# Running two gate/up blocks ahead of the first down phase, putting a state phase on 64-column halves of the array, and cutting the last tile pair in three

## Chip, cores, metric

One core of one Trainium2 chip. The metric is the device time of one execution in microseconds, median over executions; "span" is the time from the first to the last instruction in a profile, about 1.3 to 1.6 us less.

## The reference

`x` is 2048 x 640 in bfloat16; 32 heads of 20.

```python
q, k, v = split_heads(x @ wqkv)                       # 32 heads of 20
phi_q = concat(softmax(q @ w_phi), softmax(-(q @ w_phi)))
phi_k = concat(softmax(k @ w_phi), softmax(-(k @ w_phi)))
kv  = einsum("hsf,hsd->hfd", phi_k, v)                # "gram": summed over all 2048 tokens
z   = phi_k.sum(tokens)
a   = ((phi_q @ kv) / (phi_q @ z + 1e-6)) @ wo        # numerator over denominator
b   = (gelu(x @ w_gate) * (x @ w_up)) @ w_down        # 640 -> 1728 -> 640
g   = sigmoid(x . gate_w)
out = g * a + (1 - g) * b
```

## The kernel before

Tokens go in 16 tiles of 128, or 4 blocks of 512. There are three kinds of work on TensorE:

1. The state phase: for each tile t, project v and k (`vk`), exponentiate k on ScalarE, normalise it on VectorE (`k_norm`), and add the tile's outer product to the state (`gram`); between these, project q (`pq`).
2. Gate/up, 14 chunks per block: two chains of five 512-column matmuls into a pair of PSUM banks; gelu on ScalarE, product `hT` on VectorE.
3. Down, two tiles at a time, on the two 64-row halves of the array, with the attention numerators (`num(t)`, also on 64-row halves) in between. Each `num` takes 0.39 us of TensorE and then a chain of ten VectorE operations, which must end before the next `num` may write the same four banks.

The gram multiplies `vaug` (v with a column of ones, 21 columns per head) by both exponentials. Only the blocks on the diagonal (a head with itself) are wanted:

```python
def gram_groups(self):              # six groups of six heads, 126 of 128 columns used
    fe = 6 * self.DH
    for g in range(6):
        lo = min(6 * g * self.DA, self.H * self.DA - P)
        yield g, 3 + g % 2 if g < 4 else 5, 2 * fe * (g // 2 if g < 4 else g - 4), lo, fe * g, min(fe, self.D - fe * g)

def gram(self, t):
    ...
    for g, b, c, lo, f0, nf in self.gram_groups():
        sc.op("pe", lambda e: e.matmul(
            self.bank(b)[:, c:c + 2 * nf], va[:, lo:lo + P], self.Ek[:, se, :, f0:f0 + nf], ...))
```

The order of the second half (cut):

```python
early = {8: 0, 10: 1, 12: 2}                       # numerators inside gate/up of block 0
side = [{20: 3, 72: 4, 98: 5, 124: 6, 148: 7}, {40: 8, ...}, ...]   # inside the down phases
for b in range(self.NB):
    for idx, c in enumerate(order):
        self.gateup(b, c, ...)
        if b == 0:
            if idx == 0: self.gram(14)
            if idx == 3: self.gram(15); self.kv_evac(); self.gates()
            if idx == 6: self.kv_mask()
            if idx in early: self.num(early[idx])
    for t in (4 * b, 4 * b + 2):
        for step in self.down_pair(t, p, b == 0):
            if n in side[b]: self.num(side[b][n])
            step()
            n += 1
```

The state is copied out of PSUM (`kv_evac`), transposed by DMA, and spread into block-diagonal form by 4 copies and 15 multiplications on VectorE (`kv_mask`) before `num(0)`.

The softmax here doesn't subtract the row's maximum and nothing guards it: scores larger than these inputs give would overflow.

## Time and profile before

| | |
|---|---|
| time, median of 3 fast runs (of 4) | 296.9 us |
| span of the profiled run | 294.6 us |
| TensorE busy | 98% |
| VectorE / ScalarE busy | 56% / 36% |
| granted TensorE clock | 1.00 |

The head of the profile page: span, then busy time, share and instructions of each engine ("PEld" is weight loading, which overlaps "PE").

```profile
span 294.6 us, 6191 instructions
...
PE 288.2 (98%) x2608; PEld 165.5 (56%) x2608; DVE 165.6 (56%) x331; ACT 105.8 (36%) x197; POOL 27.7 (9%) x52
```

The groups of instructions with shapes kept apart, gram alone. Columns: line, engine, operation, operands, rows*columns of the array, shape, count | busy us, mean ns of one | idle before.

```profile
L441 PE MATMUL ps<-Ek,vaug 128*128 128x240 bf16 x80 | 10.7, 266 | 0.0
L441 PEld LDWEIGHTS ps<-Ek,vaug 128*128 128x128 bf16 x96 | 9.3, 98 | 2.1
L441 PE MATMUL ps<-Ek,vaug 128*128 128x80 bf16 x16 | 3.2, 199 | 0.0
```

A matmul's recorded length overlaps its neighbours, so cost is read from the distance of starts. This is the TensorE timeline before (start us, length us, engine, line, operation, count).

```profile
50.01 1.26 PE L441 MATMUL ps<-Ek,vaug 128*128 128x240 bf16 x12
...
59.23 0.71 PE L441 MATMUL ps<-Ek,vaug 128*128 128x240 bf16 x6
59.78 1.24 PE L505 MATMUL ps<-xT,wq 128*128 128x512 bf16 x5
60.86 2.87 PE L348 MATMUL ps<-w,xT 128*128 128x512 bf16 x15
63.57 0.71 PE L441 MATMUL ps<-Ek,vaug 128*128 128x240 bf16 x6
```

One gram costs 59.78 - 59.23 = 0.55 us, five 512-column matmuls 60.86 - 59.78 = 1.08 us (216 ns each), a whole tile 63.57 - 59.23 = 4.34 us. The x12 at 50.01 is grams 5 and 6 in a row, so gram 6 starts near 50.55. The VectorE timeline at the same time:

```profile
46.77 1.48 DVE L418 TENSOR_REDUCE Dk<-Ek 128x64 f32<-128x1280 bf16 x1
48.28 0.55 DVE L422 RECIPROCAL Dk<-Dk 128x64 f32<-128x64 f32 x1
48.87 1.56 DVE L427 TENSOR_TENSOR Ek<-Ek,Dk 128x640 bf16<-128x640 bf16 x2
50.35 1.48 DVE L418 TENSOR_REDUCE Dk<-Ek 128x64 f32<-128x1280 bf16 x1
```

Normalisation 6 ends near 50.4 us (48.87 + 1.56), less than 0.2 us before gram 6 begins, and the next one starts at once: VectorE is back to back here, 3.58 us per tile. The waits of TensorE (waiter <- awaited: us in total, times, longest):

```profile
PE ps L533 <- DVE zero L529: 1.3, 1, 1.3
PE ps L646 <- DVE O L673: 1.1, 3, 0.6
PE ps L700 <- DVE hT L618: 0.4, 1, 0.4
PE ps L505 <- ACT Eq L511: 0.3, 1, 0.3
PE ps L646 <- DVE KV L496: 0.3, 1, 0.3
```

The first is the start-up; the others are in block 0 (L646 is `num`, L700 is down), but for one in the state phase. By windows, the stretch from the first gram (29.40 us) to the end splits so. Columns: window, its length, busy us and instructions of PE, PEld, DVE, ACT and POOL, then the granted clock, the busy share of the DMA engines and the GB/s that they moved:

```profile
29.40:82.54 53.14, 53.14 (x331) 31.12 (x330) 49.06 (x56) 39.13 (x78) 0.00 (x0) 1.00 0.34 110
82.54:140.26 57.72, 55.68 (x604) 31.50 (x602) 42.07 (x115) 14.93 (x27) 8.79 (x7) 1.00 0.17 36
140.26:191.28 51.02, 51.02 (x515) 29.15 (x511) 23.25 (x55) 11.51 (x22) 6.56 (x5) 1.00 0.12 27
...
291.82:294.60 2.78, 0.01 (x2) 0.00 (x0) 0.55 (x1) 0.53 (x1) 0.00 (x0) 1.00 0.22 59
```

They are the state phase, block 0, block 1 and the tail after the last matmul. Block 0 takes 6.7 us more than block 1, which has neither its extra numerators, its two grams nor its waits.

### The profile page before, as it was taken

The page shows a single profiled execution, that of the slowest core. Times are in us where ns is not written, and L with a number is a line of the kernel's source. Part 1 is how long each engine was busy: PE and PEld are TensorE (multiplying, and loading weights), DVE is VectorE, ACT ScalarE, POOL GpSimd, SP SyncE. Part 2 cuts the span into 40 slices and gives each one's busy share as a digit, 9 for nine tenths or more (in the row PEclk, how much of TensorE's full clock was granted, in tenths as well). Part 3 has the DMA queues.
Part 4 walks back from the last instruction along what each step waited for, and adds up shares of the span by engine and source line. Part 5 has one row for each costly group of instructions (what it writes and reads, how often), then busy time and mean ns, then how long its engine had stood idle before and what let it go on. Part 6 is the DMA issues. An engine that isn't in the chain of part 4 may idle for free.

```text
span 294.6 us, 6191 instructions
## 1 busy us (share of the span) xinstructions
PE 288.2 (98%) x2608; PEld 165.5 (56%) x2608; DVE 165.6 (56%) x331; ACT 105.8 (36%) x197; POOL 27.7 (9%) x52
## 2 busy tenths in 40 slices
PE   8999999999999999998999999999999999999996
PEld 4675656555554444765444477744447764444774
DVE  3258999998875799458733227473237743323000
ACT  3368787586664221021322302132320223232012
POOL 7000000000000012312300001310001230000000
PEclk9999999999999999999999999999999999999999
DMA  8999992000002102113210001230000132000011
GB/s 226 213 185 313 359 346 84 0 0 2 0 2 55 34 2 46 24 24 91 78 15 0 0 2 24 70 89 2 0 0 20 29 70 67 2 0 0 2 47 45
DMA packets 38373, 18.93 MB, mean 64 GB/s; under 512 B 30154, under 2 KB 38090, under 8 KB 38346
## 3 DMA queue, kind: packets, MB, share of 16 engines
q1 hardware_dynamic: 37392, 18.11, 24.5%
q10 hardware_dynamic: 954, 0.44, 0.6%
q8 instruction: 20, 0.33, 0.5%
q14 instruction: 7, 0.06, 0.1%
HBM read 9.04 MB, written 2.62 MB: 40 GB/s over the span
## 4 chain that ended last, share of the span: by engine, by line
PE 55%; DVE 7%; issue 2%; ACT 0%; DVEq 0%
PE ps L613 29%; PE ps L700 23%; DVE O L673 2%; PE ps L646 2%; PE ps L623 1%; DVE hT L618 1%; DVE RH L667 1%; DVE RH L662 1%; DVE RH L668 1%; DVE RH L665 0%; DVE RH L663 0%; DVE RH L664 0%; DVE RH L666 0%; DVE RH L669 0%; ACT outsb L726 0%
## 5 line engine op out<-in xcount | busy, mean ns | idle before, releaser
L618 DVE TENSOR_TENSOR hT<-ps,gl 128x512 bf16<-128x512 f32 x52 | 35.6, 690 | 55.8 <-PE ps L613 55.6
L613 PE MATMUL ps<-xT,wg_sb 128*128 128x512 bf16 x260 | 64.7, 379 | 0.0
L613 PE MATMUL ps<-xT,wu_sb 128*128 128x512 bf16 x260 | 64.6, 379 | 0.0
L700 PE MATMUL ps<-wd_sb,hT 64*128 64x320 bf16 x864 | 64.0, 296 | 0.4 <-DVE hT L618 0.4
L616 ACT ACTIVATE gl<-ps 128x512 bf16<-128x512 f32 x52 | 31.1, 597 | 73.8 <-PE ps L613 67.7
L700 PEld LDWEIGHTS ps<-wd_sb,hT 64*128 64x128 bf16 x864 | 41.5, 94 | 18.1 <-ACT gl L616 0.8
L613 PEld LDWEIGHTS ps<-xT,wu_sb 128*128 128x128 bf16 x260 | 25.5, 98 | 30.6
L726 ACT ACTIVATE outsb<-ps,Gm 128x320 bf16<-128x320 f32 x31 | 14.6, 525 | 77.7 <-PE ps L700 77.6
L675 POOL TENSOR_TENSOR Og<-O,O 128x640 bf16<-128x640 bf16 x16 | 22.3, 1395 | 212.8 <-DVE O L673 212.8
L613 PEld LDWEIGHTS ps<-xT,wg_sb 128*128 128x128 bf16 x260 | 24.9, 98 | 29.4 <-issue 0.3
L348 PE MATMUL ps<-w,xT 128*128 128x512 bf16 (+3 forms) x240 | 40.9, 321 | 0.0
L348 PEld LDWEIGHTS ps<-w,xT 128*128 128x128 bf16 x240 | 22.4, 97 | 18.2
L700 PE MATMUL ps<-wo_sb,goT 64*128 64x320 bf16 x320 | 27.0, 296 | 0.0
L418 DVE TENSOR_REDUCE Dk<-Ek 128x64 f32<-128x1280 bf16 x16 | 23.7, 1481 | 3.2 <-ACT gcol L410 3.2
L427 DVE TENSOR_TENSOR Ek<-Ek,Dk 128x640 bf16<-128x640 bf16 x32 | 25.0, 821 | 0.6
L505 PE MATMUL ps<-xT,wq 128*128 128x512 bf16 x100 | 24.7, 379 | 0.3 <-ACT Eq L511 0.3
L673 DVE TENSOR_TENSOR O<-ps,RH 128x640 bf16<-128x640 f32 x32 | 24.8, 816 | 0.0
L511 ACT ACTIVATE Eq<-ps 128x512 bf16<-128x512 f32 x40 | 21.7, 604 | 4.0 <-PE ps L505 4.0
L407 ACT ACTIVATE Ek<-ps 128x640 bf16<-128x640 f32 x32 | 20.7, 702 | 3.5 <-PE ps L348 3.5
L662 DVE RECIPROCAL RH<-ps 128x32 f32<-128x32 f32 x16 | 5.7, 356 | 23.5 <-PE ps L646 23.5
L700 PEld LDWEIGHTS ps<-wo_sb,goT 64*128 64x128 bf16 x320 | 15.2, 94 | 5.7
L505 PEld LDWEIGHTS ps<-xT,wq 128*128 128x128 bf16 x100 | 8.8, 98 | 8.4 <-ACT Eq L511 0.8
(65 smaller groups left out, 150.2 us busy)
## 6 DMA issues: line engine op xcount, KB each, us to landing
out_dram<-outsb SPq DMA_DIRECT2D x14, 160.0 KB, 2.1
wd_sb<-in_B_w_down_dram SPq DMA_DIRECT2D x1, 2080.0 KB, 12.6
wg_sb<-in_B_w_gate_dram SPq DMA_DIRECT2D x1, 1120.0 KB, 6.1
wu_sb<-in_B_w_up_dram SPq DMA_DIRECT2D x1, 1120.0 KB, 9.5
wg_sb<-in_B_w_gate_dram SPq DMA_DIRECT2D x1, 960.0 KB, 9.6
wu_sb<-in_B_w_up_dram SPq DMA_DIRECT2D x1, 960.0 KB, 10.2
w<-in_A_wqkv_dram SPq DMA_DIRECT2D x5, 160.0 KB, 4.3
wo_sb<-in_A_wo_dram SPq DMA_DIRECT2D x1, 800.0 KB, 9.3
```

The costliest lines, as they stand in the source:

```text
L348: sc.op("pe", lambda e, kt=kt: e.matmul(self.bank(bank)[:, bcol:bcol + n], self.xT[:, kt, t * P:(t + 1) * P], self.w3[:, kt, c0:c0 + n], s ...
L407: self.sc.op("act", lambda e, s=s, scale=scale: e.activation(self.Ek[:, se, s, :], self.ps[:, o:o + self.D], AF.Exp, scale=scale), reads=[ ...
L418: sc.op("dve", lambda e: e.tensor_reduce(self.Dk[:, se, 0, :].rearrange("p (s h) -> p s h", h=H), self.Ek[:, se, :, :].rearrange("p s (h d ...
L427: sc.op("dve", lambda e, v=v, r=r: e.tensor_tensor(v, v, r, ALU.mult), reads=[("Rk", se)], writes=[("Ek", se, s)])
L505: sc.op("pe", lambda e, kt=kt: e.matmul(self.bank(bank), self.wq2[:, kt, i * P:(i + 1) * P], self.xT[:, kt, b * self.BT:(b + 1) * self.BT] ...
L511: sc.op("act", lambda e, s=s, scale=scale: e.activation(self.Eq[:, s, i, b * self.BT:(b + 1) * self.BT], self.bank(bank), AF.Exp, scale=sc ...
L613: sc.op("pe", lambda e, kt=kt, w=w, bk=bk: e.matmul(self.bank(bk), w[:, kt, c * P:(c + 1) * P], xs(kt), start=(kt == 0), stop=(kt == self. ...
L616: sc.op("act", lambda e: e.activation(self.gl[:, slot, :], self.bank(banks[0]), AF.Gelu_apprx_tanh), reads=[("ps", banks[0])], writes=[("g ...
L618: sc.op("dve", lambda e: e.tensor_tensor(self.hT[:, c, :], self.bank(banks[1]), self.gl[:, slot, :], ALU.mult), reads=[("ps", banks[1]), ( ...
L673: dve(lambda e, o=o, f=f, s=s: e.tensor_tensor(o, V[s][:, :, :, 0:DH], f, ALU.mult), rb + [key(6 + s)], [("O", s, sl)], guard=old)
L675: sc.op("pool", lambda e: e.tensor_tensor(self.Og[:, sl, :], self.O1[:, sl, :], self.O2[:, sl, :], ALU.add), reads=[("O", 0, sl), ("O", 1, ...
L700: sc.op("pe", lambda e: e.matmul(self.bank(bk, 320), lhs, rhs, start=first, stop=fin, skip_group_check=True), reads=rd, writes=[("ps", bk) ...
```

## The change

The intent: (a) a gram of narrower groups (three heads, 63 of 64 columns) does half the multiplications for blocks that nobody wants, if two such matmuls run at once on the two column halves of the array; (b) so that TensorE does not change its array mode between grams and projections, all projections of that stretch are cut into two 64-column halves too; (c) gate/up of blocks 0 and 1 both run before the first down phase (a second `hT`, laid over buffers of the state phase), so numerators need not be squeezed into down 0; (d) the last pair of tiles is finished in column parts of 256, 256 and 128 instead of 320 and 320, so that less is left to evict and store at the end.

```diff
+    def mm(self, bank, c0, n, lhs, rhs, first, fin, reads):
+        for a, z in ((0, 64), (64, P)) if self.columns else ((0, P),):
+            self.sc.op("pe", lambda e: e.matmul(
+                self.ps[a:z, bank * 512 + c0:bank * 512 + c0 + n], lhs[:, a:z], rhs, start=first, stop=fin),
+                reads=reads, writes=[("ps", bank)], signal=fin and z == P)
     def gram_groups(self):
-        fe = 6 * self.DH
-        for g in range(6): ...
+        fe = 3 * self.DH
+        for g in range(11):
+            u = g // 2
+            yield (g, 64 * (g % 2), 3 + u // 4, 2 * fe * (u % 4), min(3 * g * self.DA, self.H * self.DA - 64), fe * g,
+                   min(fe, self.D - fe * g))
     def gram(self, t):
-                self.bank(b)[:, c:c + 2 * nf], va[:, lo:lo + P], self.Ek[:, se, :, f0:f0 + nf],
+                self.ps[a:a + 64, b * 512 + c:b * 512 + c + 2 * nf], va[:, lo:lo + 64], self.Ek[:, se, :, f0:f0 + nf],
 ... kv_evac: one transpose instead of two; kv_mask: 20 multiplications instead of 15; proj and pq call mm ...
+        self.columns = True          # from the first gram to the end of the state phase
         self.gram(0)
 ... ffn ...
+        def state(idx):
+            if idx == 2: self.gram(14); self.gram(15); self.kv_evac(); self.gates()
+            if idx == 6: self.kv_mask()
+        def first_nums(idx):
+            if idx in (3, 6, 9, 12): self.num(idx // 3 - 1)
+        at = (8, 44, 80, 116)
+        gateups(0, state)
+        gateups(1, first_nums)
+        for b in range(self.NB):
+            downs(b, {at[k]: 4 * b + 4 + k for k in range(4)} if b < 3 else {})
+            if b < 2:
+                gateups(b + 2, none)
 ... downs, for the pair that is final ...
+                for _ in self.down_pair(t, p + [(2, 3)] if final else p, (256, 256, 128) if final else (320, 320)):
```

(The inner `if` lines are joined here. Outputs of two tiles now also leave in one DMA, and the special order of the first down phase, output projections last, is gone.)

More of the change, by code (lines that the diff above doesn't have):

```diff
@@ L134, in run @@
         self.alloc()
+        self.columns = False
         self.sc = _Sched(nc, {"sp": (nc.sync, 16), "act": (nc.scalar, 4), "pool": (nc.gpsimd, 2)})
@@ L151, in alloc @@
         self.Eq = T("Eq", [P, 2, KD, S], BF16)
-        self.Ek = T("Ek", [P, self.NSE, 2, D], BF16)
-        self.vaug = T("vaug", [P, self.NSV, self.H, self.DA], BF16)
-        self.Dk = T("Dk", [P, self.NSE, 2, 2 * self.H], F32)
         self.KV = T("KV", [P, KD, 2, self.HB * self.DB], BF16)
@@ L188, in alloc @@
             [("w3", [P, KD, 2 * D + 2], BF16), ("wq2", [P, KD, D], BF16)],
-            [("hT", [P, NFC, BT], BF16), ("gl", [P, 3, BT], BF16)],
+            [("hT0", [P, NFC, BT], BF16), ("gl", [P, 3, BT], BF16)],
+        ])
+        place([
+            [("Ek", [P, self.NSE, 2, D], BF16), ("vaug", [P, self.NSV, self.H, self.DA], BF16),
+             ("Dk", [P, self.NSE, 2, 2 * self.H], F32)],
+            [("hT1", [P, NFC, BT], BF16)],
         ])
@@ L343, in fold @@
             self.sc.op("act", lambda e: e.activation(dst, src, AF.Copy), reads=rd, writes=wr)
+    def mm(self, bank, c0, n, lhs, rhs, first, fin, reads):
[3 more added lines that the diff above has]
+                reads=reads, writes=[("ps", bank)], signal=fin and z == P)
     def proj(self, t, c0, n, bank, bcol, keys):
-        sc = self.sc
         for kt in range(self.KD):
-            sc.op("pe", lambda e, kt=kt: e.matmul(
-                self.bank(bank)[:, bcol:bcol + n], self.xT[:, kt, t * P:(t + 1) * P], self.w3[:, kt, c0:c0 + n],
-                start=(kt == 0), stop=(kt == self.KD - 1)),
-                reads=[("xT", t)] + [(k, kt) if k != "wgate" else k for k in keys],
-                writes=[("ps", bank)], signal=(kt == self.KD - 1))
+            self.mm(bank, bcol, n, self.xT[:, kt, t * P:(t + 1) * P], self.w3[:, kt, c0:c0 + n], kt == 0,
+                    kt == self.KD - 1, [("xT", t)] + [(k, kt) if k != "wgate" else k for k in keys])
     def v_step(self, t, kt):
@@ L430, in gram_groups @@
     def gram_groups(self):
-        fe = 6 * self.DH
-        for g in range(6):
-            lo = min(6 * g * self.DA, self.H * self.DA - P)
-            yield g, 3 + g % 2 if g < 4 else 5, 2 * fe * (g // 2 if g < 4 else g - 4), lo, fe * g, min(fe, self.D - fe * g)
+        fe = 3 * self.DH
[3 more added lines that the diff above has]
+                   min(fe, self.D - fe * g))
     def gram(self, t):
@@ L439, in gram, with copy @@
         va = self.vaug[:, sv, :, :].rearrange("p h c -> p (h c)")
-        for g, b, c, lo, f0, nf in self.gram_groups():
+        for g, a, b, c, lo, f0, nf in self.gram_groups():
             sc.op("pe", lambda e: e.matmul(
-                self.bank(b)[:, c:c + 2 * nf], va[:, lo:lo + P], self.Ek[:, se, :, f0:f0 + nf],
-                start=(t == 0 and g in (0, 1, 4)), stop=(t == self.NT - 1 and g in (2, 3, 5)), skip_group_check=True),
+                self.ps[a:a + 64, b * 512 + c:b * 512 + c + 2 * nf], va[:, lo:lo + 64], self.Ek[:, se, :, f0:f0 + nf],
+                start=(t == 0 and g in (0, 1, 8, 9)), stop=(t == self.NT - 1 and g in (6, 7, 9, 10)),
+                skip_group_check=True),
                 reads=[("Ek", se, 0), ("Ek", se, 1), ("vaug", sv), ("vmain", sv), ("vone", sv)], writes=[("ps", b)],
-                signal=(g in (2, 3, 5)))
+                signal=(g in (7, 10)))
     def kv_evac(self):
         sc = self.sc
-        fe = 6 * self.DH
-        def copy(ek, dst, src, rd, wr):
+        fe = 3 * self.DH
+        def copy(ek, dst, src, b):
+            rd, wr = [("ps", b)], [("Ek", 0, 0), ("Ek", 0, 1)]
             if ek == "d":
@@ L455, in copy @@
                 sc.op("act", lambda e: e.activation(dst, src, AF.Copy), reads=rd, writes=wr)
-        for pl, ek in ((0, "d"), (1, "a")):
-            f = pl * fe
-            dst = self.Ek[:, pl, :, 0:4 * fe].rearrange("p s (b c) -> p b s c", c=2 * fe)[:, :, :, f:f + fe]
-            src = self.bank(3 + pl, 4 * fe).rearrange("p (b s f) -> p b s f", f=fe, s=2)
-            copy(ek, dst, src, [("ps", 3 + pl)], [("Ek", pl, 0)])
-        for pl, ek in ((0, "d"), (1, "d")):
-            g = 4 + pl
-            nf = min(fe, self.D - fe * g)
-            src = self.bank(5)[:, pl * 2 * fe:pl * 2 * fe + 2 * nf].rearrange("p (s f) -> p s f", f=nf)
-            copy(ek, self.Ek[:, pl, :, fe * g:fe * g + nf], src, [("ps", 5)], [("Ek", pl, 1)])
-        for pl in (0, 1):
-            sc.dma("sp", lambda e: e.dma_start_transpose(
-                self.Ek[:, 2 + pl, :, :].rearrange("p s (i c) -> p (s i) c", c=P),
-                self.Ek[:, pl, :, :].rearrange("p s f -> p (s f)")),
-                reads=[("Ek", pl, 0), ("Ek", pl, 1)], writes=[("Ek", 2 + pl, 0), ("Ek", 2 + pl, 1)])
+        for q in (0, 1):
+            a, z = 64 * q, 64 * q + 64
+            dst = self.Ek[a:z, 0, :, 0:8 * fe].rearrange("p s (u q f) -> p u s q f", q=2, f=fe)[:, :, :, q, :]
+            src = self.ps[a:z, 3 * 512:3 * 512 + 8 * fe].rearrange("p (u s f) -> p u s f", s=2, f=fe)
+            copy("d", dst, src, 3)
+        for g, a, b, c, lo, f0, nf in self.gram_groups():
+            if b == 4:
+                src = self.ps[a:a + 64, b * 512 + c:b * 512 + c + 2 * nf].rearrange("p (s f) -> p s f", f=nf)
+                copy("a", self.Ek[a:a + 64, 0, :, f0:f0 + nf], src, b)
+        sc.dma("sp", lambda e: e.dma_start_transpose(
+            self.Ek[:, 2, :, :].rearrange("p s (i c) -> p (s i) c", c=P),
+            self.Ek[:, 0, :, :].rearrange("p s f -> p (s f)")),
+            reads=[("Ek", 0, 0), ("Ek", 0, 1)], writes=[("Ek", 2, 0), ("Ek", 2, 1)])
     def kv_mask(self):
@@ L480, in kv_mask @@
         self.kvk = {(i, r): [] for i in range(self.KD) for r in (0, 1)}
-        lows = {g: lo for g, b, c, lo, f0, nf in self.gram_groups()}
+        lows = {g: lo for g, a, b, c, lo, f0, nf in self.gram_groups()}
         for i in range(self.KD):
@@ L486, in kv_mask @@
                 hlo = 16 * r + 3 * i
-                for g in range(hlo // 6, (hlo + 3) // 6 + 1):
-                    h0, h1 = max(hlo, 6 * g), min(hlo + 3, 6 * g + 5)
+                for g in range(hlo // 3, (hlo + 3) // 3 + 1):
+                    h0, h1 = max(hlo, 3 * g), min(hlo + 3, 3 * g + 2)
                     nh, j0 = h1 - h0 + 1, h0 - hlo
-                    o = (j // 2) * P + h0 * self.DA - lows[g]
+                    o = (j // 2) * P + 64 * (g % 2) + h0 * self.DA - lows[g]
                     dst = self.KV[a:a + 64, i, :, j0 * self.DB:(j0 + nh) * self.DB].rearrange(
                         "p s (h c) -> p s h c", c=self.DB)[:, :, :, 0:self.DA]
-                    src = self.Ek[q:q + 64, 2 + g % 2, :, o:o + nh * self.DA].rearrange("p s (h c) -> p s h c", c=self.DA)
+                    src = self.Ek[q:q + 64, 2, :, o:o + nh * self.DA].rearrange("p s (h c) -> p s h c", c=self.DA)
                     m = self.hmask[q:q + 64, j % 2, i, j0:j0 + nh].unsqueeze(1).unsqueeze(3).to_broadcast(
@@ L496, in kv_mask @@
                     sc.op("dve", lambda e: e.tensor_tensor(dst, src, m, ALU.mult),
-                          reads=[("Ek", 2 + g % 2, 0), ("hmask", j % 2), ("KVd", r, 0), ("KVd", r, 1)],
+                          reads=[("Ek", 2, 0), ("hmask", j % 2), ("KVd", r, 0), ("KVd", r, 1)],
                           writes=[("KV", i, r, g)])
@@ L504, in pq @@
         for kt in range(self.KD):
-            sc.op("pe", lambda e, kt=kt: e.matmul(
-                self.bank(bank), self.wq2[:, kt, i * P:(i + 1) * P], self.xT[:, kt, b * self.BT:(b + 1) * self.BT],
-                start=(kt == 0), stop=(kt == self.KD - 1)),
-                reads=[("xT", t) for t in range(4 * b, 4 * b + 4)] + [("wq2", kt)],
-                writes=[("ps", bank)], signal=(kt == self.KD - 1))
+            self.mm(bank, 0, 512, self.wq2[:, kt, i * P:(i + 1) * P], self.xT[:, kt, b * self.BT:(b + 1) * self.BT],
+                    kt == 0, kt == self.KD - 1, [("xT", t) for t in range(4 * b, 4 * b + 4)] + [("wq2", kt)])
         for s, scale in ((0, 1.0), (1, -1.0)):
@@ L605, in gateup @@
         xr = [("xT", t) for t in range(4 * b, 4 * b + 4)]
-        oldw = self.oldw
+        oldw, hT = (self.oldw, self.hT0) if b % 2 == 0 else (self.oldk, self.hT1)
+        hk = b % 2
         slot = self.gn % 3
@@ L616, in gateup @@
             sc.op("act", lambda e: e.activation(self.gl[:, slot, :], self.bank(banks[0]), AF.Gelu_apprx_tanh),
-                  reads=[("ps", banks[0])], writes=[("gl", slot)], guard=oldw)
-            sc.op("dve", lambda e: e.tensor_tensor(self.hT[:, c, :], self.bank(banks[1]), self.gl[:, slot, :], ALU.mult),
-                  reads=[("ps", banks[1]), ("gl", slot)], writes=[("hT", c)], guard=oldw)
+                  reads=[("ps", banks[0])], writes=[("gl", slot)], guard=self.oldw)
+            sc.op("dve", lambda e: e.tensor_tensor(hT[:, c, :], self.bank(banks[1]), self.gl[:, slot, :], ALU.mult),
+                  reads=[("ps", banks[1]), ("gl", slot)], writes=[("hT", hk, c)], guard=oldw)
         else:
@@ L627, in gateup @@
                                                 AF.Gelu_apprx_tanh),
-                  reads=[("ps", bk)], writes=[("gl", slot)], guard=oldw)
+                  reads=[("ps", bk)], writes=[("gl", slot)], guard=self.oldw)
             for r in (0, 1):
@@ L631, in gateup @@
                 sc.op("dve", lambda e: e.tensor_tensor(
-                    odd(self.hT[64 * r:64 * r + 64, c, :]), odd(self.ps[64:128, bk * 512:bk * 512 + 512]),
+                    odd(hT[64 * r:64 * r + 64, c, :]), odd(self.ps[64:128, bk * 512:bk * 512 + 512]),
                     odd(self.gl[64:128, slot, :]), ALU.mult),
-                    reads=[("ps", bk), ("gl", slot)], writes=[("hT", c, r)], guard=oldw)
+                    reads=[("ps", bk), ("gl", slot)], writes=[("hT", hk, c, r)], guard=oldw)
     def num(self, t):
@@ L679, in num, with down_pair, mm @@
                reads=[("Og", sl)], writes=[("goT", gs)], guard=old)
-    def down_pair(self, t0, banks, late):
+    def down_pair(self, t0, banks, widths):
         sc = self.sc
         ts = (t0, t0 + 1)
-        bank = {(j, h): banks[h][j] for j in (0, 1) for h in (0, 1)}
         NFC, KD = self.NFC - 1, self.KD
+        nw = len(widths)
+        hk = t0 // 4 % 2
+        hT = (self.hT0, self.hT1)[hk]
         last = t0 + 2 == self.NT
-        done = {}
-        def mm(r, j, h, c, first, fin, wait, end):
+        os_ = t0 % 4
+        def mm(r, j, h, c, opens, x, n):
@@ L691, in mm @@
             t = ts[j]
-            tt, gs, bk, w0, a = t % 4, t % 8, bank[j, h], 320 * h, 64 * r
+            tt, gs, bk, w0, a = t % 4, t % 8, banks[h][j], sum(widths[:h]), 64 * r
+            w, end = widths[h], x == n - 1
             if c <= NFC:
-                lhs, rhs = self.hT[a:a + 64, c, tt * P:(tt + 1) * P], self.wd_sb[a:a + 64, c, w0:w0 + 320]
-                rd = [("hT", c), "wd"] if c < NFC else [("hT", 13, r), ("wd13", r)]
+                lhs, rhs = hT[a:a + 64, c, tt * P:(tt + 1) * P], self.wd_sb[a:a + 64, c, w0:w0 + w]
+                rd = [("hT", hk, c), "wd"] if c < NFC else [("hT", hk, 13, r), ("wd13", r)]
@@ L696, in mm @@
             else:
                 k = c - NFC - 1
-                lhs, rhs = self.goT[a:a + 64, gs, k, :], self.wo_sb[a:a + 64, k, w0:w0 + 320]
+                lhs, rhs = self.goT[a:a + 64, gs, k, :], self.wo_sb[a:a + 64, k, w0:w0 + w]
                 rd = [("goT", gs), "wo"]
-            sc.op("pe", lambda e: e.matmul(self.bank(bk, 320), lhs, rhs, start=first, stop=fin, skip_group_check=True),
+            sc.op("pe", lambda e: e.matmul(self.bank(bk, w), lhs, rhs, start=opens and x == 0, stop=end and not opens,
+                                           skip_group_check=True),
@@ L701, in mm @@
                   reads=rd, writes=[("ps", bk)] + ([("turn", bk)] if end else []), signal=end,
-                  after=[("turn", bk)] if wait else ())
-        def part(q, cs, opens, fin):
-            h = q % 2
-            n = len(cs)
-            for x, c in enumerate(cs):
-                def step(x=x, c=c):
-                    for r in (0, 1):
-                        j = r if q < 2 else 1 - r
-                        mm(r, j, h, c, opens and x == 0, fin and x == n - 1, x == 0 and not opens, x == n - 1)
-                    if fin and x == n - 1:
-                        for j in (0, 1):
-                            evac(j, h)
-                yield step
@@ L717, in evac @@
-        def evac(j, h):
-            t = ts[j]
-            os_, bk, w0 = t % 4, bank[j, h], 320 * h
-            dst = self.outsb[:, os_, w0:w0 + 320]
-            rd, wr = [("ps", bk), "Gm"], [("outsb", os_, h)]
-            g = self.Gm[:, t:t + 1]
-            if last and h == 1 and j == 1:
-                sc.op("dve", lambda e: e.tensor_scalar(dst, self.bank(bk, 320), g, None, op0=ALU.mult), reads=rd, writes=wr)
-            else:
-                sc.op("act", lambda e: e.activation(dst, self.bank(bk, 320), AF.Copy, scale=g), reads=rd, writes=wr)
-            rows = self.out[t * P:(t + 1) * P, :]
-            if t < self.TB:
-                rows = self.out[0:self.BT, :].rearrange("(p j) n -> p j n", j=self.TB)[:, t, :]
-            if last:
-                sc.dma("act" if h == 1 and j == 0 else "sp", lambda e: e.dma_start(rows[:, w0:w0 + 320], dst),
-                       reads=wr, writes=[("out", t, h)])
-            elif h == 1:
-                sc.dma("sp", lambda e: e.dma_start(rows, self.outsb[:, os_, :]),
-                       reads=[("outsb", os_, k) for k in (0, 1)], writes=[("out", t)])
@@ L737, in down_pair @@
-        hs, ws = list(range(NFC + 1)), [NFC + 1 + k for k in range(KD)]
-        if late:
-            hs = [NFC] + hs[:NFC]
-            plan = [(q, hs if q < 2 else hs[1:], q < 2, False) for q in range(4)] + [(q, ws, False, q >= 2) for q in range(4)]
-        else:
-            plan = [(q, (hs if q < 2 else hs[:NFC]) + ws, q < 2, q >= 2) for q in range(4)]
-        for q, cs, opens, fin in plan:
-            yield from part(q, cs, opens, fin)
+                  after=[("turn", bk)] if x == 0 and not opens else ())
@@ new lines, in evac @@
+        def evac(h):
+            w0, w = sum(widths[:h]), widths[h]
+            for j in (0, 1):
+                bk, dst, g = banks[h][j], self.outsb[:, os_ + j, w0:w0 + w], self.Gm[:, ts[j]:ts[j] + 1]
+                rd, wr = [("ps", bk), "Gm"], [("outsb", os_ + j, h)]
+                if last and j == 1:
+                    sc.op("dve", lambda e: e.tensor_scalar(dst, self.bank(bk, w), g, None, op0=ALU.mult), reads=rd, writes=wr)
+                else:
+                    sc.op("act", lambda e: e.activation(dst, self.bank(bk, w), AF.Copy, scale=g), reads=rd, writes=wr)
+            if last:
+                hs, c0, c1 = [h], w0, w0 + w
+            elif h == nw - 1:
+                hs, c0, c1 = range(nw), 0, self.D
+            else:
+                return
+            if t0 < self.TB:
+                rows = self.out[0:self.BT, :].rearrange("(p j) n -> p j n", j=self.TB)[:, t0:t0 + 2, :]
+            else:
+                rows = self.out[t0 * P:(t0 + 2) * P, :].rearrange("(j p) n -> p j n", p=P)
+            sc.dma("sp", lambda e: e.dma_start(rows[:, :, c0:c1], self.outsb[:, os_:os_ + 2, c0:c1]),
+                   reads=[("outsb", os_ + j, k) for j in (0, 1) for k in hs], writes=[("out", t0, h)])
@@ L746 @@
+        for q in range(2 * nw):
+            h, opens = q % nw, q < nw
+            cs = list(range(NFC + 1 if opens else NFC)) + [NFC + 1 + k for k in range(KD)]
+            for x, c in enumerate(cs):
+                for r in (0, 1):
+                    mm(r, r if opens else 1 - r, h, c, opens, x, len(cs))
+                if x == len(cs) - 1 and not opens:
+                    evac(h)
+                yield None
     NUMB = 2
+    oldk = [("Ek", k, r) for k in range(4) for r in (0, 1)] + [(w, k) for w in ("Dk", "Rk") for k in range(4)] + [
+        (w, k) for w in ("vaug", "vmain", "vone") for k in range(8)]
@@ L751, in ffn, with gateups @@
         self.pn = 0
+        self.columns = False
         pairs = [(0, 1), (6, 7)]
-        order = [0, 1, 13] + list(range(2, 13))
-        early = {8: 0, 10: 1, 12: 2}
-        side = [{20: 3, 72: 4, 98: 5, 124: 6, 148: 7}, {40: 8, 72: 9, 110: 10, 148: 11}, {0: 12, 36: 13, 72: 14, 108: 15}, {}]
-        for b in range(self.NB):
-            for idx, c in enumerate(order):
+        def gateups(b, after):
+            for idx, c in enumerate([0, 1, 13] + list(range(2, 13))):
                 if c == 13:
@@ L762, in ffn, with downs @@
                     self.pn += 1
-                if b == 0:
-                    if idx == 0:
-                        self.gram(14)
-                    if idx == 3:
-                        self.gram(15)
-                        self.kv_evac()
-                        self.gates()
-                    if idx == 6:
-                        self.kv_mask()
-                    if idx in early:
-                        self.num(early[idx])
+                after(idx)
+        def downs(b, side):
             p = [pairs[(self.pn + k) % 2] for k in (0, 1)]
@@ L776, in ffn, with none @@
             for t in (4 * b, 4 * b + 2):
-                for step in self.down_pair(t, p, b == 0):
-                    if n in side[b]:
-                        self.num(side[b][n])
-                    step()
+                final = t + 2 == self.NT
+                for _ in self.down_pair(t, p + [(2, 3)] if final else p, (256, 256, 128) if final else (320, 320)):
                     n += 1
-            if n in side[b]:
-                self.num(side[b][n])
+                    if n in side:
+                        self.num(side[n])
+        def state(idx):
+            if idx == 2:
+                self.gram(14)
+                self.gram(15)
+                self.kv_evac()
+                self.gates()
+            if idx == 6:
+                self.kv_mask()
+        def first_nums(idx):
+            if idx in (3, 6, 9, 12):
+                self.num(idx // 3 - 1)
+        def none(idx):
+            pass
+        at = (8, 44, 80, 116)
[5 more added lines that the diff above has]
+                gateups(b + 2, none)
 def bass_gated_mix__linear_kernel_hedgehog__geglu_ffn__prompt_kernel(
```

## The prediction

> **What bounds it.** TensorE. The page's busy table gives PE 98% of the 294.6 us span, DVE 56%, ACT 36%; the granted clock is 1.0 throughout. In the PE timeline five 512-column matmuls take 1.08 us (216 ns each), and a pair of 64-row, 320-column down matmuls 136 ns, so weight loads are hidden and PE runs at its column rate. The waits view finds only 3.4 us of PE idling. By windows: state phase to 82.5 us; block 0 from 82.5 to 140.3 (57.7 us); later blocks 29.25 us gate/up plus 21.8 us down.
>
> **Losses that the change addresses.**
> 1. Gram: six matmuls per token tile, 0.545 us, 16 times = 8.7 us.
> 2. Block 0: pieces at rate sum to 53.5 us (27 gate/up groups of 1.08, 8 numerators of 0.39, 296 down matmuls of 0.068, two grams). About 4.2 us is lost: numerator 0 waits on KV (1.1), down waits on the last hT (0.6), three late numerators wait on the DVE chain (0.5, 0.5, 0.8), array mode changes about 0.1 us each.
>
> **After.** Gram becomes eleven 64-wide matmuls of 120 (80) columns, two at once: by the pair rule seen in the down phase about 0.30 us, saving 0.245 each, 3.9 us in all. The projections double in count but should stay at 216 ns per 512-column pair, if each half's weight load hides. The Trainium skill ("TensorEngine Tiling (Array Packing)", Restrictions and Gotchas) says column tiling excludes Fast Weight Load; whether that shows is this prediction's main doubt, and no trace before has a 64-column load. Loads of 64 columns easily fit under 216 ns, but a 120-column pair has only about 52 ns; if loads serialise there, gram saves little.
>
> DVE takes part of the gram gain back. Its k-normalisation runs back to back at 3.58 us per tile from 25.3 to 64.7 us; gram 6 already starts only 0.2 us after its normalisation (50.35 us). A faster PE reaches it about 1.3 us early and waits. So the state phase should gain about 2.2 us, not 3.7. Grams 14 and 15, now together between 128-wide gate/ups, gain 0.5 less 0.2 for two mode changes.
>
> Block 0 and the run-ahead: the KV wait, the hT wait and the bunched numerators go. New costs: the KV masking becomes 20 DVE operations instead of 15 (about 4.9 instead of 3.95 us) with no numerator behind it, so gate/up group 9's second half waits about 1.6 us for hT; four numerators inside gate/up cost two mode changes each (0.8 us, before three: 0.6); the first numerator in down 0 waits about 0.6 us for the previous one's DVE chain. Net gain about 1 us. There are two fewer gate/up–down boundaries (0.2 us).
>
> Tail: last evacuation 128 instead of 320 columns, about 0.1 us less; a third part costs 37 more pairs at about 2.5 ns. Near zero.
>
> **Prediction.** Gain about 3.5 us: 293.4 us, range 290.3 to 298.5. Faster by over 2%: 0.12; within 2%: 0.81; slower: 0.07.
>
> **What would show it.** Right: gram at about 0.30 us, vk tiles at a 4.1 us period, a PE wait on DVE of 1 to 1.5 us at gram 6 and of 1 to 2 us in gate/up 0, no DVE waits in later blocks, 29.25 and 21.8 us for undisturbed stages. Wrong: 512-column pairs above 216 ns, or gram at 0.5 us or more.
>
> **What would make it wrong.** Exposed weight loads on 64-column halves: 245 projection pairs at +50 ns would cost 12 us and make it slower. Better than predicted if the two DVE waits are shorter than I worked out.

## More of the kernel before

Two executions were much slower (507.92 us of the kernel before, 426.85 us of one experiment); no time here is taken from them, and where something is read from them, the text says so.

## The result, and the profile after

The changed kernel took 291.94 us (four runs, 291.52 to 292.19) against 296.86 us, the median of the three fast runs of the kernel before: ratio 0.984, interval 0.9815 to 0.9864, within 2%. In a second session it was 0.9835. A ratio is the mean time of one kernel's fast runs over that of the other's fast runs of the same rounds, so it is not quite the ratio of the medians quoted. Executions over 1.5% slower than the fastest of the same kernel are left out of the means. The measured time lies in the predicted range (290.3 to 298.5) and below the predicted middle (293.4).

The page's head, and the gram's groups, after:

```profile
span 290.6 us, 6966 instructions
...
PE 282.1 (97%) x2990; PEld 179.2 (62%) x3007; DVE 167.5 (58%) x337; ACT 105.2 (36%) x199; POOL 27.6 (10%) x52
```

```profile
L449 PE MATMUL ps<-Ek,vaug 128*64 128x120 bf16 x160 | 7.6, 216 | 1.2 <-DVE Ek L433 1.2
L449 PEld LDWEIGHTS ps<-Ek,vaug 128*64 128x64 bf16 x176 | 7.6, 109 | 2.6 <-DVE Ek L433 1.3 <-issue 0.4 <-DVE hT L625 0.4
```

A 64-column weight load is recorded longer (109 ns) than the 128-column one before (98 ns). It is not exposed, as the TensorE timeline after shows:

```profile
49.14 0.57 PE L449 MATMUL ps<-Ek,vaug 128*64 128x120 bf16 x11
50.90 0.46 PE L449 MATMUL ps<-Ek,vaug 128*64 128x120 bf16 x11 [1.19 <-DVE Ek L433]
51.19 1.25 PE L351 MATMUL ps<-xT,wq 128*64 128x512 bf16 x10
52.27 2.88 PE L351 MATMUL ps<-w,xT 128*64 128x512 bf16 x30
54.97 0.43 PE L449 MATMUL ps<-Ek,vaug 128*64 128x120 bf16 x10
```

Ten 512-column matmuls on halves take 52.27 - 51.19 = 1.08 us, as five did on the full width. A gram takes 51.19 - 50.90 = 0.29 us. And gram 6 has the wait in brackets: 1.19 us for `Ek`, the normalisation. The waits of TensorE after:

```profile
PE ps L538 <- DVE zero L534: 1.3, 1, 1.3
PE ps L449 <- DVE Ek L433: 1.2, 1, 1.2
PE ps L620 <- DVE hT L625: 1.0, 1, 1.0
...
PE ps L653 <- DVE O L680: 0.4, 1, 0.4
```

So one wait at gram 6, one in the gate/up of block 0 (for `hT`), one at the first numerator of down 0. (Waits put down to "issue", 1.0 us in six of 0.16 us in this view and in that of the last run below, and the 0.2 us for `gcol`, stand where a chain shows four matmuls instead of five, its first record missing; the control's profile has all five in those places, and no such wait.) By windows, after:

```profile
29.85:81.03 51.18, 49.99 (x645) 44.10 (x646) 48.88 (x56) 38.54 (x78) 0.00 (x0) 1.00 0.38 123
...
166.38:217.40 51.02, 50.76 (x509) 29.04 (x512) 23.35 (x55) 12.16 (x23) 5.58 (x5) 1.00 0.13 27
...
288.45:290.60 2.15, 0.00 (x2) 0.00 (x0) 0.35 (x1) 0.37 (x1) 0.00 (x0) 1.00 0.34 92
```

Where the time came from, first gram to end of span:

| stretch | before | after | gain |
|---|---|---|---|
| state phase, from the first gram | 53.14 | 51.18 | 1.96 |
| all gate/up, grams 14 and 15, numerators, down | 209.28 (82.54 to 291.82) | 207.42 (81.03 to 288.45) | 1.86 |
| tail after the last matmul | 2.78 | 2.15 | 0.63 |
| sum | 265.20 | 260.75 | 4.45 |

In the profile after, the first record of the first gate/up is missing. In the control's profile it is there, and the state phase is 80.48 - 29.37 = 51.11 us, so that the first gain is 2.0 us. An undisturbed stage of gate/up and down is the same to a hundredth (51.02 us in both), so the gain is where the change put it.

The part before the first gram is not touched by the change, but it varies from run to run: the first gram starts at 29.37 to 30.41 us in eleven profiles. Below, "from the first gram" is the span less that start; the changed kernel has 260.75 and, in the second session, 290.1 - 29.37 = 260.73.

### The profile page after: what moved, and what is told of

Its sections match the earlier page's. It is cut to its first block, busy times and chain, and to the rows that moved or that the text cites. A ratio compares the mean times of both kernels' runs of the same rounds, so it can differ in the third digit from the quotient of the medians.

```text
span 290.6 us, 6966 instructions
## 1 busy us (share of the span) xinstructions
PE 282.1 (97%) x2990; PEld 179.2 (62%) x3007; DVE 167.5 (58%) x337; ACT 105.2 (36%) x199; POOL 27.6 (10%) x52
## 4 chain that ended last, share of the span: by engine, by line
PE 82%; DVE 8%; SPq 3%; issue 3%; DMA 2%; ACT 2%; ACTq 0%
PE ps L620 36%; PE ps L710 27%; PE ps L351 13%; DVE Dk L424 2%; PE ps L653 2%; DVE Ek L433 2%; DMA xT<-in_A_x_dram 2%; PE ps L630 1%; SPq L220 1%; DVE KV L504 1%; PE ps L449 1%; DVE Dk L428 1%; ACT Ek L413 1%; PE ps L331 1%; SPq L224 1%
## 5 line engine op out<-in xcount | busy, mean ns | idle before, releaser
L710 PE MATMUL ps<-wd_sb,hT 64*128 64x320 bf16 (+2 forms) x918 | 66.3, 288 | 0.0
L620 PE MATMUL ps<-xT,wg_sb 128*128 128x512 bf16 x250 | 62.9, 379 | 1.3 <-issue 1.0
L710 PEld LDWEIGHTS ps<-wd_sb,hT 64*128 64x128 bf16 x918 | 42.8, 94 | 15.4 <-ACT gl L623 0.8
L723 ACT ACTIVATE outsb<-ps,Gm 128x320 bf16<-128x320 f32 (+2 forms) x31 | 14.6, 516 | 75.3 <-PE ps L710 75.3
L351 PE MATMUL ps<-w,xT 128*64 128x512 bf16 (+6 forms) x398 | 41.4, 325 | 0.2
L351 PEld LDWEIGHTS ps<-w,xT 128*64 128x64 bf16 (+1 forms) x400 | 33.4, 107 | 7.3 <-DMA xT<-in_A_x_dram 0.2
L710 PE MATMUL ps<-wo_sb,goT 64*128 64x320 bf16 (+2 forms) x340 | 27.3, 288 | 0.0
L351 PE MATMUL ps<-xT,wq 128*64 128x512 bf16 (+1 forms) x184 | 25.8, 380 | 0.4 <-ACT Eq L516 0.3
L710 PEld LDWEIGHTS ps<-wo_sb,goT 64*128 64x128 bf16 x340 | 16.2, 94 | 5.6
L351 PEld LDWEIGHTS ps<-xT,wq 128*64 128x64 bf16 (+1 forms) x185 | 14.5, 108 | 4.1 <-ACT Eq L516 0.8
```

The source lines that it names most:

```text
L351: self.sc.op("pe", lambda e: e.matmul(self.ps[a:z, bank * 512 + c0:bank * 512 + c0 + n], lhs[:, a:z], rhs, start=first, stop=fin), reads=r ...
L620: sc.op("pe", lambda e, kt=kt, w=w, bk=bk: e.matmul(self.bank(bk), w[:, kt, c * P:(c + 1) * P], xs(kt), start=(kt == 0), stop=(kt == self. ...
L710: sc.op("pe", lambda e: e.matmul(self.bank(bk, w), lhs, rhs, start=opens and x == 0, stop=end and not opens, skip_group_check=True), reads ...
L723: sc.op("act", lambda e: e.activation(dst, self.bank(bk, w), AF.Copy, scale=g), reads=rd, writes=wr)
```

## The experiments

Theory: TensorE is the limit at its column rate; the gram is cheaper because two column halves run at once; the halved projections only avoid mode changes; and the three waits on VectorE are real losses. Rivals stand with each run.

> The changed kernel unaltered, as the control on the same chip as the next three. Expected 0.984 of the kernel before (about 292 us).

Measured: 291.38 us, ratio 0.9835 (0.9817 to 0.9853). 

### Grams on halves, projections not

```diff
         self.pq(0, 3, 3)
-        self.columns = True
         self.gram(0)
```

> Changed kernel, but only the grams use 64-column halves; the projections of the state phase stay 128 columns wide. Theory (halving the projections is only there to avoid array mode changes, and costs nothing itself): each of the 13 gram places pays two mode changes of about 0.1 us, 2.6 us of TensorE time in all, of which the 1.2 us wait for VectorE at gram 6 hides about 1.2, so about 1.4 us slower than the changed kernel, and the wait at gram 6 nearly gone. Rival A (halved projections have a cost of their own, because their weight loads are slower): equal or faster than the changed kernel. Rival B (changes between 128x128 and 128x64 are free): equal.

Measured: 293.75 us, ratio 0.9905; 2.4 us over the control, of which 1.6 us from the first gram (292.4 - 30.09 = 262.3) and the rest before it. Gram 6 does not wait. The TensorE timeline of this run:

```profile
59.71 0.48 PE L449 MATMUL ps<-Ek,vaug 128*64 128x120 bf16 x11
60.13 1.25 PE L351 MATMUL ps<-xT,wq 128*128 128x512 bf16 x5
61.22 2.87 PE L351 MATMUL ps<-w,xT 128*128 128x512 bf16 x15
64.02 0.48 PE L449 MATMUL ps<-Ek,vaug 128*64 128x120 bf16 x11
```

From gram to gram it is 4.31 us, against 4.34 before and 4.05 to 4.09 with everything on halves. A pair of mode changes therefore costs 4.31 less about 4.08, some 0.23 us, nearly all of the 0.26 us that the narrow gram saves. Halving the projections is what makes (a) pay. Both rivals fall: neither are mode changes free nor do halved projections cost anything.

### The old gram in the changed kernel

The edit puts `gram_groups`, `gram`, `kv_evac` and `kv_mask` of the kernel before back, and never sets `columns`.

> Changed kernel with the old gram: six 128-wide matmuls, two transposes, the 15-operation masking, no halves anywhere. Isolates the run-ahead and the tail. Theory: the state phase loses its 1.9 us, grams 14 and 15 cost 1.09 instead of 0.80 us, the masking wait in gate/up 0 shrinks by about 0.3; together 1.9 us slower than the changed kernel, about 0.990 of the kernel before. Rival (the halves brought nothing on balance and the gain is all run-ahead and tail): equal to the changed kernel.

Measured: 293.45 us, ratio 0.9902 (0.9887 to 0.9916); 2.1 us over the control, 2.0 from the first gram (292.2 - 29.46 = 262.7). As expected; the wait for `hT` shrank from 1.0 to 0.7 us. Run-ahead and tail alone are thus worth about 2.9 us against the kernel before, 2.5 of them from the first gram (265.2 less 262.7).

### One half after the other

```diff
-        for g, a, b, c, lo, f0, nf in self.gram_groups():
+        for g, a, b, c, lo, f0, nf in sorted(self.gram_groups(), key=lambda x: (x[1], x[0])):
...
-                signal=(g in (7, 10)))
+                signal=(g in (7, 9)))
```

> Changed kernel, the same eleven gram matmuls, but all of one column half first and then all of the other. Theory (the gram is faster only because two halves run at once): gram back to 0.45 to 0.53 us, 0.2 us more for each of 16, of which the wait at gram 6 hides up to 1.2: 1.6 to 2.2 us slower than the changed kernel, and the wait at gram 6 gone. Rival (the halves stream one after the other in any case, the gain is in shorter or fewer loads): no change.

Measured: 292.51 us, ratio 0.9869, 1.1 us over the control; but from the first gram only 0.3 us (291.4 - 30.41 = 261.0), and gram 6 still waits 1.0 us. The expectation missed: the gram hardly became longer. The timeline shows why not:

```profile
55.53 0.51 PE L449 MATMUL ps<-Ek,vaug 128*64 128x120 bf16 x10
55.83 0.38 PE L351 MATMUL ps<-xT,wq 128*64 128x512 bf16 x1
55.88 0.21 PE L449 MATMUL ps<-Ek,vaug 128*64 128x120 bf16 x1
```

The start times of that gram's matmuls, taken from the trace, in us:

```
first half,  issued 1st to 6th:  55.531 55.584 55.637 55.689 55.742 55.794
second half, issued 7th to 11th: 55.643 55.722 55.774 55.827 55.879
```

The second half's first matmul, issued seventh, starts before the fourth: the halves do not keep the issue order between them, they run ahead of each other, and reordering the instructions did not take their concurrency away. This run could therefore not tell the theory from its rival. Most of its 1.1 us lies before the first gram, in code that is the same. In its profile the transposes of `x` at the start, up to the first projection, take 1.98 us against 1.19 in the control: most of them start 107 ns apart, in the control nearly all 56 ns apart. That is 0.8 of the 1.0 us by which this front is longer. Only one of its four runs was profiled; why the other three were as long, is open.

### All grams on one half

Wrong result on purpose (the groups are accumulated on 64 partitions in three banks, and evicted as before).

```diff
-                self.ps[a:a + 64, b * 512 + c:b * 512 + c + 2 * nf], va[:, lo:lo + 64], ...
+                self.ps[0:64, 1536 + 512 * (g // 4) + 120 * (g % 4):1536 + 512 * (g // 4) + 120 * (g % 4) + 2 * nf], ...
```

> Wrong result on purpose: the changed kernel with all eleven gram matmuls on the same 64 columns, so that no two of a gram can run at once; count, sizes and weight loads stay. The run with the halves in turn could not tell this, since the halves still overlapped in its trace. Theory (the gain is two halves at once): gram 0.56 us, 0.28 more for each of 16, less the 1.2 us wait at gram 6 that it hides: 3.2 us slower than the changed kernel from the first gram to the end, and no wait at gram 6. Rival (the gain is in shorter loads or pipelining of narrow matmuls, on one half too): less than 0.5 us slower.

Measured: 294.46 us, ratio 0.9931 (0.9916 to 0.9946; the changed kernel's was 0.9835); from the first gram 294.1 - 30.38 = 263.7, 3.0 us more than the control. Two grams in a row in its timeline:

```profile
51.10 1.20 PE L449 MATMUL ps<-Ek,vaug 128*64 128x120 bf16 x20
52.08 0.40 PE L351 MATMUL ps<-xT,wq 128*64 128x512 bf16 x1
52.13 0.25 PE L449 MATMUL ps<-Ek,vaug 128*64 128x120 bf16 x2
```

The starts within a gram are 52.5 ns apart throughout, 0.56 us in all, and no gram waits on VectorE. That is the theory's number: on one half the narrow gram costs what the old one did (0.55 us), so its saving comes from two halves at once. It also shows that a 64-column load hides under a 120-column matmul on the same columns: half of the old gram's 102.5 ns for 240 columns would be 51 ns.

### The half-array state phase alone

The kernel before with only (a) and (b).

> The kernel before with the half-array state phase alone (grams, halved projections, one transpose, 20-operation masking), with the old order of gate/up and down and the old tail. Theory (the parts add up): the state phase gains 1.9 us with the wait at gram 6, grams 14 and 15 apart among 128-wide matmuls gain nothing (0.28 plus 0.24 for two mode changes against 0.545), numerator 0 waits 0.3 us longer for the masking: 1.6 us faster than the kernel before, about 0.9945. With the 2.9 us that the version with the old gram kept, that would make 4.5 of the 4.9 us. Rival (the halves pay only together with the run-ahead): within 0.5 us of the kernel before.

Measured: 294.39 us, ratio 0.9930 (0.9916 to 0.9944), 2.1 us faster than the kernel before; from the first gram 293.0 - 29.55 = 263.45, 1.75 us better. The parts multiply to 0.9930 x 0.9902 = 0.9833, the whole is 0.9835: within the intervals (0.0014 to 0.0018 either way) they add up. Gram 6 waits 1.2 us here too.

### The last pair in two parts

```diff
-                for _ in self.down_pair(t, p + [(2, 3)] if final else p, (256, 256, 128) if final else (320, 320)):
+                for _ in self.down_pair(t, p, (320, 320)):
```

> Changed kernel with the last tile pair in two parts of 320 columns instead of 256, 256, 128. In the profiles the span ran on for 2.78 us after the last matmul's recorded end before the change and 2.15 us after it. Theory (the short last part shortens evacuation and write-out): tail back to about 2.7 us, less 0.1 us for 37 fewer matmul pairs: 0.5 us slower than the changed kernel. Rival (the tail gain is chance of one profile, or comes from one store for both tiles, which this run keeps): within 0.2 us of the changed kernel.

Measured: three fast runs, 292.04 to 292.73 us, ratio 0.9853 (0.9838 to 0.9868), 0.5 us over the changed kernel's 0.9835 (of another session, and the intervals overlap). The profile: TensorE was slowed but not the other engines (an eviction of 320 columns took 0.53 us as always); its tail is 425.6 - 422.9 = 2.7 us. So the time agrees with the theory. In this one slow profile the tail follows the width of the last part, though the store for both tiles at once was kept; no fast profile shows it, and the time alone would not settle it.

### The three waits, one by one and together

Grams one tile later until tile 13:

```diff
-                    for g in range(g, t - 2 if t < 8 else t - 1):
+                    for g in range(g, t - 2 if t < 13 else t - 1):
                         self.gram(g)
-                    g = t - 2 if t < 8 else t - 1
+                    g = t - 2 if t < 13 else t - 1
```

> Changed kernel with each gram of the middle of the state phase issued one token tile later, until tile 13, so that gram 6 no longer comes before its normalisation is done. Theory (the 1.2 us wait on VectorE at gram 6 is real loss): that wait goes, no other comes in its place, 1.1 us faster than the changed kernel. Rival (VectorE is the limit of the whole state phase, the wait only moves): equal, with a wait of about 1.2 us at a later gram.

Measured: 290.44 us, ratio 0.9791 (0.9777 to 0.9805); from the first gram 289.7 - 30.25 = 259.45, 1.3 us better than the changed kernel. No gram waits. VectorE is not the limit of the phase; it only sat in front of one gram. It is close behind, though: in the state phase of the run with all three changes below (29.65 to 79.60 us) it is busy for 48.62 of 49.95 us.

Masking spread over six gate/up groups:

```diff
         for i in range(self.KD):
+            yield
             for r in (0, 1): ...
...
             if idx == 6:
-                self.kv_mask()
+                self.masking = self.kv_mask()
+            if idx >= 6:
+                next(self.masking, None)
```

> Changed kernel with the 24 masking operations of KV spread over six gate/up groups instead of queued in one piece. Theory (the 1.0 us wait of the gate/up of block 0 is VectorE busy with masking when hT is due): that wait goes, 1.0 us faster than the changed kernel. Rival (the wait is for ScalarE or for the transpose of KV): unchanged.

Measured: 291.24 us, ratio 0.9804 (0.9789 to 0.9819); from the first gram 290.0 - 30.40 = 259.6, 1.1 us better (the interval of its ratio just touches the control's). The wait for `hT` is gone.

All three, with the first numerator of down 0 eight steps later:

```diff
-            downs(b, {at[k]: 4 * b + 4 + k for k in range(4)} if b < 3 else {})
+            downs(b, {at[k] + (8 if b == 0 and k == 0 else 0): 4 * b + 4 + k for k in range(4)} if b < 3 else {})
```

> Changed kernel with the later grams, the spread masking and the first numerator of the first down phase 8 steps later (against its 0.4 us wait on the previous numerator). If the waits are independent: 1.1 + 1.0 + 0.4 = 2.5 us faster than the changed kernel, near 289 us or 0.975 of the kernel before, with no TensorE wait on VectorE left after the warm-up. If VectorE is the limit: less than half of that.

Measured: 289.00 us (288.78 to 289.23), ratio 0.9741 (0.9728 to 0.9754), correct; from the first gram 287.5 - 29.65 = 257.85, 2.9 us better than the changed kernel. This version beats both kernels, and the kernel before by over 2%. Its waits of TensorE, whole:

```profile
PE ps L539 <- DVE zero L535: 1.3, 1, 1.3
PE ps L621 <- issue: 1.0, 6, 0.2
PE ps L290 <- DMA xtok<-in_A_x_dram: 0.5, 1, 0.5
PE ps L351 <- ACT Eq L517: 0.3, 1, 0.3
PE ps L621 <- ACT gcol L416: 0.2, 1, 0.2
```

No wait on VectorE is left after the start. The late numerator was not run by itself; its 0.4 us is read from the wait that went.

## Why the prediction was right

It was right in its range and in nearly every step; its middle was 1.5 us too slow.

- **TensorE at its column rate, halved projections free: right.** 1.08 us for ten half-width 512-column matmuls, as for five full ones. The doubt it rested on, the Trainium skill's statement that column tiling excludes Fast Weight Load ("TensorEngine Tiling (Array Packing)", Restrictions and Gotchas), may have left a trace (109 instead of 98 ns for half the columns; no run isolates it) but cost no time even at 120 columns.
- **Gram: right.** 0.30 us expected, about 0.27 to 0.29 seen; the run on one half gave 0.56 us.
- **Part of it lost to VectorE at gram 6: right.** 1.3 us expected, 1.19 seen; 1.3 us came back when grams went one tile later. State phase: 2.2 us gain expected, 1.96 measured.
- **Masking wait: right in kind, mis-sized.** 1.6 us expected from 4.9 us of multiplications; the VectorE timeline shows the 20 of them in 4.29 us, and the wait was 1.03 us. The queue was 0.6 us shorter than expected, and so was the wait. The recorded lengths of the 20 add up to 4.79 us, but they overlap.
- **First numerator of down 0: right.** 0.6 us expected, 0.41 seen.
- **Block 0 and run-ahead together:** about 1.5 us expected (1 net, 0.2 for boundaries, 0.3 for grams 14 and 15), 1.86 measured; the two waits that were shorter (by 0.57 and 0.2 us) make up more than the 0.36 us between them, so about 0.4 us of the other estimates was too high; which, was not traced.
- **Tail: the term most in error.** "Near zero" was written; 0.63 us was measured after the last matmul, less about 0.1 us for the extra pairs (an estimate: matmuls of 240 columns start 102.5 ns apart and those of 512 columns 216, which leaves about 2.4 ns for each, whatever its width; 37 pairs make 0.09 us). The last evictions fell from 0.53 and 0.55 us to 0.37 and 0.35 us, where 0.1 us had been allowed, and the end of the last store came about 0.5 us sooner after them (290.60 - 288.89 = 1.7 against 294.60 - 292.42 = 2.2 us). The store was taken as fixed; two stores of 80 KB had become one of 64 KB.
- The rest of the 1.5 us lies outside these terms. From the first gram the two profiles differ by 4.45 us, the times by 4.9; the front varies by up to a microsecond between runs, and the part of the time outside the span is 1.3 us after and 1.6 us before. No run was made to explain either. The pace of the transposes at the start (see the run with the halves in turn) is one part of the front's spread, but not what sets these two profiles apart: they take 1.52 us before and 1.13 us after, while the first gram comes 0.45 us later after.

## What to carry to other kernels

When an engine is made faster in a phase that it bounds, look for the engine right behind it and ask where it has the least slack: here a slack of less than 0.2 us at one gram took 1.2 us of an estimated gain of 3.9, and moving that gram by one tile gave it back. The narrower array mode paid here only because its neighbours ran in the same mode: one visit to the other mode cost 0.23 us, almost the whole saving of one visit. And changes that are each under 2% can be told apart when each sits in its own stretch of the bottleneck: undo them one at a time and multiply the ratios.

## What the Trainium skill lacked or had wrong

- "TensorE: Matmul & The Clock Gate", Part 3, What overlaps and what doesn't, says that matmuls start and end strictly in program order, and that one increment on the last tile's matmul is therefore sound. Not so between two column halves here: with one half's matmuls issued first, the seventh started at 55.643 us, before the fourth at 55.689. In a projection of the control (257 columns, five matmuls on each half), the half that carries the increment started its last matmul at 78.785 us and the other half, issued first, its own at 78.899, 0.11 us later. Both runs gave correct results, but the increment of one half does not by itself show the other half's end.
- The same section says that weight loads overlap running matmuls only where the row group differs (a little earlier, under The mechanism, it also lets a load go ahead into a background weight buffer, which fits what was seen). On one and the same 64 columns and all 128 rows, 120-column matmuls with a load each started 52.5 ns apart, about what 120 columns take alone, with loads recorded at 109 ns: they overlap.
- "TensorEngine Tiling (Array Packing)", Key Properties, says that a mode change drains TensorE but not for how long. There and back between 128x128 and 128x64 cost 0.23 us (4.31 instead of about 4.08 us per tile); in the changed kernel a `num` between two gate/up groups takes 0.6 us from the one to the other, where `num` alone takes 0.39.
- The same page, Restrictions, lists the loss of Fast Weight Load under column tiling without its cost ("TensorE: Matmul & The Clock Gate", Part 2, has a figure for that mode, about twofold): 109 ns recorded for 64 columns against 98 ns for 128, none of it exposed.
- "TensorE: Matmul & The Clock Gate", Part 4, reports that the full clock does not engage for transposes. The 20 transposes at the start ran 56 ns apart in the profile of the changed kernel, and 107 ns apart until 6.6 us, then 56, in the run with the halves in turn. The page's Part 1 (a free-running warm-up window whose phase varies) agrees in kind with such a spread; the profile's granted clock showed 1.0 for both.
- No page describes a state of a single-core program in which TensorE runs at about two thirds of its pace with the granted clock recorded as 1.000: the 320-column down matmuls were 99 ns apart instead of 68 in the 426.85 us run.
